# Performer attention and an MLP on one core: the seven-product form in all of block 7, a new sequence, and other engines for the scaled v rows

## The chip, the cores and the metric

One Trainium2 chip, one core of it. The kernel is a single launch: attention and the MLP that follows it, from the inputs in DRAM to the output in DRAM. The metric is device time in microseconds (us) of the slowest core, which here is the only one. Lower is better.

The engines are named as in the profile: PE is TensorE (PEld its weight loads), DVE is VectorE, ACT is ScalarE, POOL is GpSimd, SP is SyncE. SP, ACT and POOL issue DMAs.

## The reference

Eight batches (B), eight heads (H), 576 tokens (S), head size 64 (D), 128 random features (M). Attention is linear: queries and keys become positive features, and the keys are summed against the values once per head.

```python
def phi(x):
    proj = np.einsum('bhsd,md->bhsm', x, omega)
    sq = np.sum(x * x, axis=-1, keepdims=True) / 2.0
    h = proj - sq
    h = h - np.max(h, axis=-1, keepdims=True)
    return np.exp(h) / np.sqrt(m)

q_p, k_p = phi(q * D**-0.25), phi(k * D**-0.25)
kv  = np.einsum('bhsm,bhsd->bhmd', k_p, v)
z   = np.sum(k_p, axis=2)
num = np.einsum('bhsm,bhmd->bhsd', q_p, kv)
den = np.einsum('bhsm,bhm->bhs', q_p, z)[..., None] + 1e-06
x   = (num / den).transpose(0, 2, 1, 3).reshape(4608, 512)

h = x @ w_in                                   # 512 -> 2048
g = h * np.clip(h + 3.0, 0.0, 6.0) / 6.0
out = g @ w_out                                # 2048 -> 512
```

## The kernel before

**How the work is written down.** Each step is an `op` of a small planner (`Prog`): the engines that may do it, a cost, the function that emits its instructions, and the keys that it reads and writes. Steps have running numbers. A table `ORDER` lists, for each of the five engines, the numbers of its steps in sequence; an engine works its list strictly in that sequence. `schedule` replays the table with the planner's costs. It decides two things only: which of the eight PSUM banks a step gets, and how many fill matmuls (named `idle`, without use for the result) PE is given in the first 21 us (`IDLE_UNTIL`). `emit` turns the dependencies into semaphore waits. So the sequence on every engine is fixed ahead of the run, DMA issues included, and a step whose data are late holds up everything that is behind it on its engine.

**Attention, by batch.** A batch's 576 tokens are 512 main ones and 64 left over; pairs of heads share the 128 partitions. `load` (L619) issues the DMAs: in batch 0 SP and ACT issue k, q and v as f32 (pieces k00, k10, ..., q11, v11, and the left-over rows kl, ql, vl); in later batches POOL issues k and q as casting DMAs to bf16, and SP issues v. k and q are transposed (PE and DVE or ACT in batches 0 and 1, DMA from batch 2 on), PE projects them on omega (L808; L764 and L767 in the row-tiled form from batch 3 on), ACT takes the exponentials (L815, L783, L832, L792), and DVE takes the row maxima of the key features (L819, L788). The reciprocal of the maximum, `cc`, scales the v rows that belong to it:

- `vc` scales the 512 main rows of a pair of heads. On POOL it is one instruction (L924), on ACT eight (L926). `EV_VC` allows POOL or ACT in batches 1 to 7, `V0` gives POOL or DVE in batch 0.
- `vcl` (L851) scales the left-over rows, in two halves per batch: on DVE in batch 0, on POOL after it.

For each pair of heads PE then forms kv and z (L940, eight matmuls on `vc` and one on `vcl`, copied to `kvz`) and the numerator with its denominator (L968); DVE takes the reciprocal (L980) and divides (L984). The result goes to `xb` and is transposed to `xT`: by PE in batches 0 and 1, by a DMA that SP issues (L1013, `Xdma`) from batch 2 on. The left-over tokens of all batches are collected in `xS`.

**The MLP, by block.** Block b is the 512 main tokens of batch b; block 8 is the 8 x 64 left-over tokens. w_in comes in five casting DMAs from POOL (`w_in_piece`: wi0 in two parts, wi1, wi2, wi3, each 512 of the 2048 columns), gated by the landing of q11; w_out comes in eight. Block 0's first product is done in token halves (`mm1_half`, L1181). Blocks 1 to 8 use one of two forms for h = x @ w_in:

- `mm1` (L1037): for one of 16 column tiles four matmuls of 128 x 512, then a relu on ACT (L1043) and a multiplication on DVE (L1045).
- `mm1_pair`: two column tiles f and f+8 at once. The product is seen as a 2 x 2 by 2 x 2 block product and is done with seven block products for eight. PE issues 14 matmuls of 256 columns (L1116) in stages a, b, c, d. Between the stages are three copies on ACT (`s1` L1144, `s3` L1146, `s2` L1149) and two adds on DVE (`a2` L1152, `a1` L1154). The relu and the multiplication (L1163, L1165) follow twice.

The pair form needs sums of blocks of w_in (`input_sums`: W1 to W4, once per half of the column tiles, on DVE) and of x (`x_sums`: X1 to X4, once per block, on DVE or POOL). Which tiles use it is set by

```python
    FIRST7 = (8, 7)
    ...
    def seven(blk, f):
        return blk >= FIRST7[f // 4]
```

so in block 7 the pairs f = 4 to 7 use it and f = 0 to 3 do not; in block 8 all use it.

The second product, g @ w_out, of blocks 1 to 8 is in a seven-product form as well (`products`, L1290, outputs combined by `plus` L1306), on sums of w_out (T1 to T4) and on sums of g (`token_sums` and `last_sum`: S1 to S4, four groups per block). The sums of g, like those of x, go through `combine` (L1222); those of g are on POOL in every block. Block 0's second product is plain (L1206). The last product of block 8 is split into three parts so that its output leaves in pieces (`last_product`: L1356, adds C12.8 L1364, DMAs `outl` L1368). The other outputs leave by `store` (L1383).

**What sets the order around the change.** The table alone. The steps are interleaved far across batches: while PE works on block b, the engines prepare batches b+1 and b+2. In the first 21 us PE has little real work, since data are still landing, and the MLP of block 0 begins as soon as batch 0's first pairs of heads are through.

Of the kernel before, what the change touches and what calls it, by code (L numbers as in the profile page):

```python
# [15 lines left out]
EV0 = (("ACT","DVE"), ("ACT","DVE"), ("POOL","DVE"), {"k": ("POOL", "ACT", "DVE"), "q": ("POOL", "ACT","DVE")})  # L16
# [4 lines left out]
        13, 118, 139, 124, 150, 115, 144, 156, 162, 147, 153, 127, 121, 168, 133, 159, 130, 177, 175, 183, 136, 165,  # L21
        197, 212, 185, 199, 179, 142, 181, 219, 214, 204, 227, 202, 229, 171, 187, 242, 173, 217, 189, 232, 409, 415,
        244, 410, 411, 222, 207, 254, 416, 249, 257, 247, 417, 234, 403, 404, 405, 406, 412, 252, 418, 421, 237, 424,
        427, 430, 433, 436, 439, 282, 280, 442, 300, 303, 288, 445, 260, 448, 451, 284, 306, 286, 321, 454, 315, 312,
        318, 296, 309, 294, 457, 324, 292, 583, 290, 573, 574, 331, 339, 298, 329, 575, 584, 585, 343, 353, 337, 576,
        333, 327, 586, 577, 366, 341, 335, 587, 358, 355, 578, 379, 345, 368, 579, 371, 392, 588, 381, 394, 589, 397,
        384, 590, 374, 361, 593, 580, 387, 594, 400, 595, 596, 597, 621, 624, 630, 642, 627, 598, 636, 639, 654, 651,
        645, 657, 480, 599, 492, 666, 603, 477, 501, 604, 483, 605, 489, 672, 511, 660, 507, 600, 474, 503, 486, 606,
        505, 607, 513, 498, 509, 675, 517, 669, 495, 515, 608, 609, 782, 798, 610, 792, 539, 783, 519, 544, 527, 541,
        785, 529, 532, 786, 551, 793, 563, 695, 556, 553, 568, 795, 796, 565, 799, 702, 801, 802, 723, 805, 806, 709,  # L30
        809, 815, 812, 736, 818, 741, 824, 830, 827, 842, 833, 716, 839, 748, 863, 738, 860, 848, 854, 857, 845, 750,
        772, 980, 774, 760, 753, 970, 971, 762, 765, 986, 777, 973, 974, 981, 883, 890, 983, 984, 987, 897, 989, 990,
        911, 993, 1003, 997, 1000, 1012, 1015, 924, 1006, 926, 994, 1018, 929, 1021, 1030, 1027, 1033, 1042, 904, 936,
        1045, 1036, 1048, 1051, 938, 1168, 960, 1174, 941, 1158, 1159, 1071, 962, 948, 965, 1161, 1169, 950, 953,
        1162, 1171, 1078, 1172, 1175, 1085, 1177, 1178, 1092, 1181, 1191, 1185, 1112, 1194, 1200, 1117, 1188, 1203,
        1206, 1209, 1215, 1218, 1224, 1221, 1099, 1233, 1230, 1236, 1136, 1182, 1124, 1239, 1129, 1346, 1347, 1356,
        1148, 1126, 1114, 1349, 1141, 1138, 1153, 1150, 1350, 1357, 1362, 1287, 1359, 1259, 1360, 1363, 1266, 1365,
        1366, 1273, 1388, 1379, 1391, 1376, 1300, 1369, 1373, 1312, 1305, 1403, 1314, 1397, 1317, 1382, 1406, 1394,
        1302, 1336, 1409, 1412, 1338, 1370, 1421, 1418, 1424, 1280, 1427, 1341, 1534, 1535, 1544, 1454, 1537, 1538,
        1324, 1447, 1545, 1461, 1550, 1547, 1329, 1326, 1548, 1551, 1468, 1553, 1557, 1554, 1488, 1475, 1500, 1567,  # L40
        1502, 1490, 1558, 1579, 1493, 1512, 1561, 1505, 1524, 1591, 1576, 1526, 1514, 1517, 1570, 1529, 1582, 1600,
        1615, 1594, 1609, 1564, 1606, 1612, 1597, 1585, 1686, 1659, 1662, 1677, 1671, 1656, 1680, 1625, 1674, 1689,
        1699, 1626, 1691, 1665, 1702, 1628, 1694, 1635, 1704, 1629, 1715, 1636, 1707, 1728, 1718, 1641, 1720, 1638,
        1748, 1639, 1731, 1723, 1779, 1733, 1644, 1782, 1645, 1784, 1736, 1792, 1749, 1642, 1795, 1787, 1808, 1797,
        1648, 1811, 1649, 1800, 1821, 1813, 1751, 1824, 1752, 1826, 1816, 1837, 1758, 1829, 1850, 1840, 1759, 1853,
        1842, 1764, 1855, 1765, 1845, 1866, 1858, 1879, 1761, 1869, 1882, 1762, 1871, 1884, 1905, 1767, 1874, 1887,
        1768, 1895, 1771, 1772, 1896, 1911, 1906, 1898, 1899, 1908, 1909, 1912, 1915, 1916, 1924, 1932, 1928,
    ],
    "SP": [
        0, 21, 17, 22, 23, 32, 19, 24, 25, 31, 26, 27, 28, 29, 30, 269, 271, 270, 469, 470, 471, 468, 472, 473, 402,  # L50
        582, 467, 691, 692, 592, 602, 693, 694, 612, 547, 535, 690, 559, 689, 571, 688, 804, 572, 880, 879, 882, 808,
        881, 878, 756, 744, 877, 876, 768, 780, 781, 1067, 932, 992, 1069, 1064, 996, 1070, 1068, 1065, 968, 1066,
        944, 956, 969, 1180, 1255, 1256, 1258, 1184, 1257, 1253, 1120, 1144, 1132, 1252, 1156, 1254, 1368, 1157, 1440,
        1320, 1443, 1445, 1372, 1446, 1444, 1442, 1441, 1344, 1308, 1332, 1345, 1560, 1556, 1508, 1496, 1520, 1532,
        1533, 1647, 1651, 1774, 1770, 1918, 1935, 1927, 1931, 1930,
    ],
    "ACT": [
        18, 20, 123, 119, 140, 151, 145, 148, 163, 157, 129, 154, 135, 128, 134, 196, 141, 160, 211, 178, 166, 176,
        169, 184, 186, 226, 182, 180, 228, 241, 172, 203, 243, 190, 174, 188, 208, 223, 248, 407, 419, 413, 422, 425,
        253, 428, 238, 434, 431, 283, 437, 440, 443, 301, 304, 446, 449, 261, 452, 287, 307, 322, 316, 313, 310, 455,  # L60
        297, 293, 319, 352, 291, 325, 299, 458, 340, 344, 354, 378, 330, 365, 328, 332, 334, 338, 391, 336, 342, 346,
        380, 393, 388, 362, 401, 622, 625, 631, 581, 628, 640, 637, 643, 591, 655, 646, 481, 493, 658, 667, 502, 652,
        478, 484, 490, 512, 508, 661, 487, 475, 504, 506, 510, 514, 499, 518, 670, 516, 673, 537, 611, 676, 526, 540,
        496, 784, 520, 550, 561, 562, 787, 552, 564, 701, 696, 698, 705, 700, 708, 707, 703, 728, 724, 710, 712, 810,
        714, 715, 816, 746, 813, 819, 729, 825, 831, 726, 747, 828, 834, 719, 843, 717, 840, 721, 770, 849, 771, 855,
        759, 861, 846, 864, 722, 858, 972, 975, 886, 891, 884, 893, 888, 895, 889, 896, 900, 898, 902, 922, 914, 917,
        1004, 923, 998, 912, 1001, 1016, 1013, 916, 1007, 903, 1019, 1022, 1031, 1028, 1034, 1043, 905, 907, 1046,
        909, 1037, 958, 1049, 910, 1052, 946, 1160, 1072, 1074, 1077, 1076, 1163, 1081, 1083, 1079, 1084, 1086, 1090,
        1110, 1088, 1095, 1111, 1093, 1097, 1192, 1098, 1186, 1134, 1189, 1195, 1204, 1201, 1091, 1207, 1216, 1135,
        1210, 1219, 1225, 1222, 1234, 1105, 1100, 1237, 1102, 1231, 1125, 1146, 1240, 1348, 1137, 1104, 1288, 1290,  # L70
        1293, 1265, 1292, 1262, 1260, 1264, 1267, 1271, 1269, 1272, 1274, 1278, 1276, 1279, 1299, 1380, 1310, 1392,
        1377, 1374, 1313, 1335, 1389, 1383, 1404, 1398, 1395, 1337, 1410, 1407, 1413, 1422, 1419, 1425, 1283, 1281,
        1285, 1286, 1428, 1322, 1457, 1455, 1460, 1459, 1448, 1450, 1539, 1462, 1464, 1466, 1467, 1486, 1469, 1453,
        1452, 1474, 1471, 1473, 1499, 1478, 1476, 1511, 1481, 1568, 1523, 1480, 1580, 1513, 1562, 1525, 1571, 1583,
        1592, 1595, 1601, 1565, 1607, 1577, 1616, 1613, 1688, 1586, 1660, 1598, 1687, 1663, 1672, 1681, 1610, 1675,
        1657, 1690, 1700, 1701, 1627, 1695, 1666, 1703, 1678, 1630, 1717, 1716, 1697, 1710, 1719, 1708, 1729, 1724,
        1730, 1732, 1780, 1781, 1726, 1737, 1783, 1739, 1793, 1794, 1788, 1796, 1810, 1809, 1801, 1790, 1812, 1803,
        1822, 1823, 1817, 1825, 1819, 1839, 1830, 1838, 1832, 1851, 1852, 1841, 1854, 1753, 1859, 1848, 1846, 1868,
        1867, 1881, 1880, 1861, 1870, 1883, 1888, 1875, 1877, 1890, 1897, 1900, 1922, 1923, 1920, 1921, 1926, 1919,
        1934,  # L80
    ],
    "DVE": [
        16, 10, 7, 5, 12, 8, 11, 14, 138, 15, 4, 6, 125, 116, 152, 146, 149, 194, 122, 164, 155, 158, 191, 209, 192,
        193, 161, 224, 198, 131, 167, 213, 200, 170, 143, 239, 201, 215, 137, 220, 216, 230, 205, 231, 218, 206, 233,
# [316 lines left out]
def _emit(nc, es, q, k, v, omega, w_in, w_out, out):  # L401
# [109 lines left out]
    def dvet(n):  # L511
        return 0.07 + n / 960.0
# [508 lines left out]
    def mm1(blk, f):  # L1021
# [13 lines left out]
        def e(E):  # L1035
# [11 lines left out]
           t - 0.1, reads=[vh, ("t", tu)], writes=[("gT", gu, f, x) for x in range(2)], name="g.%d.%d" % (blk, f))  # L1047


    FIRST7 = (8, 7)  # L1050
    XADD = ("DVE", "POOL")
    AHEAD = 2
    LAG = 0.0
# [422 lines left out]
```

## Time and profile before

| | |
|---|---|
| Median of 4 runs | 308.24 us (307.27 to 309.17) |
| The profiled execution's own time | 309.17 us |
| Its span in the trace | 307.4 us |
| Granted TensorE clock, mean | 1.00 |
| Share of the span busy | PE 97%, DVE 79%, POOL 76%, ACT 70% |
| DMA | 44.88 MB, mean 146 GB/s |
| Fill matmuls | 56 |

The profiled execution is the slowest of the four; 1.8 us of its time lie outside the span. In a row of the groups, the first number behind the bar is the busy time of all instructions of that line and shape, the second the mean of one in nanoseconds; behind the second bar stands the engine's idle time just before them and what ended most of it. A row of the waits gives the waiting instruction, what ended the wait, and the time: sum, number, longest. A row of the chain gives the start, the length and the work. A row of the stages gives the interval, its length and for each engine the busy time with the number of instructions, then the granted clock, the mean share of the DMA engines and the GB/s.

### The profile page before, as it was taken

To read this page: it belongs to the slowest core of one execution; us is meant where nothing else is said; L and a number is where in the kernel's file an instruction comes from. 1 tells how busy PE (TensorE), PEld (TensorE's weight loads), DVE (VectorE), ACT (ScalarE), POOL (GpSimd) and SP (SyncE) were. 2 spreads that over 40 slices of the span, in tenths; PEclk is the share of its full clock that TensorE was granted. 3 is DMA by queue.
4 is the path that set the end of the run, shared out by engine and by line. 5 is a ranking of instruction groups with operands and counts; after the bars stand their busy time and mean duration, and the time that the engine had idled before them with its cause. 6 is when DMAs were issued, how large, how long until landed. Compare 5 with 4: busy or idle time off the path is not lost.

```text
span 307.4 us, 7302 instructions
## 1 busy us (share of the span) xinstructions
PE 298.8 (97%) x2767; PEld 209.7 (68%) x2767; DVE 242.3 (79%) x532; ACT 213.9 (70%) x518; POOL 232.7 (76%) x247
## 2 busy tenths in 40 slices
PE   7989999999998999999999999999999999999994
PEld 5767966445885468655864686557864478888883
DVE  3797898689886987788778878798698988978833
ACT  3886896579967984969699738769764766577410
POOL 2772769089895979889869894998941999899991
PEclk9999999999999999999999999999999999999999
DMA  8999998999799996499969996999834000030045
GB/s 223 272 167 177 265 195 126 207 210 170 178 174 185 131 227 159 95 137 210 228 176 121 146 218 137 152 162 227 126 139 78 2 0 2 1 139 1 2 162 113
DMA packets 90147, 44.88 MB, mean 146 GB/s; under 512 B 57984, under 2 KB 87808, under 8 KB 90112
## 3 DMA queue, kind: packets, MB, share of 16 engines
q1 hardware_dynamic: 62096, 30.68, 44.3%
q0 software_dynamic: 26592, 12.46, 32.8%
q10 hardware_dynamic: 1424, 1.28, 1.7%
q8 instruction: 22, 0.36, 0.5%
q14 instruction: 13, 0.11, 0.1%
HBM read 36.73 MB, written 9.44 MB: 150 GB/s over the span
## 4 chain that ended last, share of the span: by engine, by line
PE 81%; DMA 8%; DVE 5%; ACT 3%; issue 0%; SPq 0%; POOL 0%; DVEq 0%; POOLq 0%
PE p L1037 29%; PE p L1290 26%; PE p L1116 6%; PE p L1206 4%; PE p L1181 3%; DMA wi<-in_moe_w_in_dram 3%; PE p L968 3%; PE p L940 2%; DMA v<-in_v_dram 2%; PE p L808 2%; DMA xT<-xb 2%; PE p L764 2%; DMA k<-in_k_dram 2%; ACT vc L926 1%; PE p L828 1%; DVE mx L819 1%
## 5 line engine op out<-in xcount | busy, mean ns | idle before, releaser
L1037 PE MATMUL p<-xT,wi 128*128 128x512 f16 x416 | 96.2, 379 | 0.8 <-DMA xT<-xb 0.8
L1045 DVE SCALAR_TENSOR_TENSOR gT<-tsb,p 128x512 f16<-128x512 f16 x104 | 67.4, 678 | 14.1 <-ACT tsb L1043 13.3
L1043 ACT ACTIVATE tsb<-p 128x512 f16<-128x512 f32 x104 | 59.9, 599 | 24.2 <-PE p L1037 16.5
L1037 PEld LDWEIGHTS p<-xT,wi 128*128 128x128 f16 x416 | 39.2, 98 | 43.2 <-DMA xT<-xb 1.1
L1222 POOL TENSOR_TENSOR s<-gT 128x512 f16<-128x512 f16 x32 | 37.7, 1179 | 15.0 <-DVE gT L1045 12.1
L1290 PE MATMUL p<-wo,gT 128*128 128x256 f16 x368 | 45.9, 273 | 0.0
L1222 POOL TENSOR_TENSOR s<-gT,s 128x512 f16<-128x512 f16 x32 | 37.0, 1156 | 4.0 <-DVE gT L1045 1.8
L1222 POOL TENSOR_TENSOR gT<-gT 128x512 f16<-128x512 f16 x32 | 37.4, 1170 | 2.4
L1222 POOL TENSOR_TENSOR gT<-gT,s 128x512 f16<-128x512 f16 x32 | 37.3, 1165 | 2.5
L1290 PEld LDWEIGHTS p<-wo,gT 128*128 128x128 f16 x368 | 34.6, 98 | 5.2 <-issue 0.8
L788 DVE TENSOR_REDUCE mx<-kp 128x4 f32<-128x512 bf16 (+1 forms) x50 | 29.8, 623 | 7.2 <-ACT kp L783 7.0
L783 ACT ACTIVATE kp<-p 128x512 bf16<-128x512 f32 (+1 forms) x50 | 26.1, 554 | 12.6 <-PE p L767 11.9
L1290 PE MATMUL p<-t,gT 128*128 128x256 f16 x256 | 32.3, 273 | 0.0
L984 DVE TENSOR_TENSOR xb<-p,rec 128x256 f16<-128x256 f32 (+1 forms) x64 | 28.9, 471 | 0.6
L926 ACT ACTIVATE vc<-v,cc 128x64 bf16<-128x64 f32 x104 | 26.3, 347 | 2.5 <-DMA v<-in_v_dram 1.4
L792 ACT ACTIVATE qpT<-p 128x512 bf16<-128x512 f32 (+1 forms) x50 | 26.4, 562 | 2.2 <-PE p L968 2.1
L1290 PEld LDWEIGHTS p<-t,gT 128*128 128x128 f16 x256 | 24.3, 98 | 4.5 <-issue 0.8
L924 POOL TENSOR_TENSOR vc<-v,cc 128x512 bf16<-128x512 f32 x19 | 20.9, 1098 | 5.4 <-DVE cc L918 3.6
L619 POOL DMA_DIRECT2D qb<-in_q_dram x28 | 19.5, 706 | 3.3 <-DMA wi<-in_moe_w_in_dram 3.1
L1163 ACT ACTIVATE tsb<-p 128x512 f16<-128x512 f32 x24 | 14.0, 600 | 8.9 <-DVE p L1152 5.1
L968 PEld LDWEIGHTS p<-kvz,qpT 128*128 128x128 bf16 x312 | 15.3, 98 | 6.5 <-issue 0.3
L819 DVE TENSOR_REDUCE mx<-kp 128x4 f32<-128x512 bf16 x27 | 17.5, 674 | 1.9 <-ACT kp L815 1.8
(129 smaller groups left out, 552.6 us busy)
## 6 DMA issues: line engine op xcount, KB each, us to landing
v<-in_v_dram SPq DMA_DIRECT2D x14, 512.0 KB, 4.8
out_dram<-osb SPq DMA_DIRECT2D x14, 512.0 KB, 2.9
kb<-in_k_dram POOLq DMA_DIRECT2D x14, 256.0 KB, 4.9
qb<-in_q_dram POOLq DMA_DIRECT2D x14, 256.0 KB, 6.0
wo<-in_moe_w_out_dram POOLq DMA_DIRECT2D x8, 256.0 KB, 7.7
wi<-in_moe_w_in_dram POOLq DMA_DIRECT2D x3, 512.0 KB, 8.2
q<-in_q_dram SPq DMA_DIRECT2D x4, 256.0 KB, 5.6
vl<-in_v_dram SPq DMA_DIRECT2D x8, 128.0 KB, 4.5
```

What stands on the lines that cost most here:

```text
L783: op("ACT", actt(128 * (d1 - d0)), lambda E, lh=lh, ko=ko, part=part: E.activation(ko, out_of(part, 0, lh)[0].rearrange("p (x m) -> p x m" ...
L788: op("DVE", dvet(128 * (d1 - d0)), lambda E, ko=ko, mo=mo: E.reduce_max(mo, ko, axis=AX.X), p0 + 0.01, reads=[("kp", 0, d, lh) for d in ra ...
L792: op("ACT", actt(128 * (d1 - d0)), lambda E, lh=lh, part=part: E.activation(qd[:, part[0]:part[1], lh, :], out_of(part, 1, lh)[0].rearrang ...
L924: return E.tensor_tensor(vcm[:, :, 0:D], v32[:, m, :, :], cbc, ALU.mult)
L926: ins = E.activation(vcm[:, i, 0:D], v32[:, m, i, :], AF.Copy, scale=cc[pb][:, c0 + i:c0 + i + 1])
L968: ins = E.matmul(d[:, hh, i - i0, :], qpT[pb][:, o:o + 128], kvz[m][:, 65 * hh:65 * hh + 65], start=True, stop=True)
L984: op("DVE", dvet(128 * n), lambda E: E.tensor_tensor(xv(i0, i1), psum()[:, :, :, 0:64], rbc, ALU.mult), t + 0.01, reads=[vn, ("rec", ru)], ...
L1037: ins = E.matmul(ring.t[vh.slot], wi[:, c, 128 * f:128 * f + 128], xv[:, c, :], start=(c == 0), stop=(c == NJ - 1))
L1043: op("ACT", actt(512), lambda E: E.activation(tsb[tu][:], ring.t[vh.slot], AF.Relu, bias=0.5, scale=1.0 / 6.0), t - 0.1, reads=[vh], write ...
L1045: op("DVE", dvet(512), lambda E: E.scalar_tensor_tensor(gT[gu][:, f, :], tsb[tu][:], 1.0, ring.t[vh.slot], ALU.min, ALU.mult), t - 0.1, re ...
L1222: op(engines, {"POOL": 0.07 + n / 455.0, "DVE": 0.1 + n / 850.0}, lambda E: E.tensor_tensor(dst, x, y, ALU.subtract if minus else ALU.add) ...
L1290: ins = E.matmul(ring.t[v.slot][:, 256 * j:256 * j + 256], a[:, f, 128 * j:128 * j + 128], w[:, f, :], start=(first and f == 0 and j == 0) ...
```

## The change

It has five parts.

1. `FIRST7` becomes (7, 7): in block 7 the pairs f = 0 to 3 use the seven-product form too. The sums W1 to W4 of the first half are therefore needed before block 7 rather than before block 8, and the sums of x for block 7 are placed like those of block 8.
2. The copies s1, s2 and s3 of a pair may be on ACT or DVE (`EV_O`); a key `seed` keeps s3 behind s1. The dependency that held a pair behind the last stage of the pair before the last (`last7[-AHEAD]`) is left out.
3. `vcl` may be on POOL or ACT. On ACT it is four activations per half. `V0` allows POOL or ACT for `vc` in batch 0.
4. Sums of g of block 8, groups 2 and 3, may be on POOL or DVE; the new table puts five of them on DVE: S3 of groups 2 and 3, and S1, S2 and S4 of group 3. Five sums of x (X2 and X4 of block 7, X1, X3 and X4 of block 8) go from DVE to POOL.
5. The planner's latency for batch 0's loads is 1.4 us for 1.0 and their issue 0.52 for 0.47, and `ORDER` is a new table for all five engines. The number of fill matmuls that follows from it is 63 for 56. The store of block 7's first rows also reads the keys that the last adds of block 8 write, so that these wait for it.

```diff
-EV0 = (("ACT","DVE"), ("ACT","DVE"), ("POOL","DVE"), {"k": ("POOL", "ACT", "DVE"), "q": ("POOL", "ACT","DVE")})
+EV0 = (("ACT","DVE"), ("ACT","DVE"), ("POOL", "ACT"), {"k": ("POOL", "ACT", "DVE"), "q": ("POOL", "ACT","DVE")})
 ORDER = {
...
 }
@@ load
-               group="d" + part + ("c" if cast else "") + (str(pb) if b and part != "v" else ""), inc=16, lat=1.0,
-               name="%s.%d" % (part, b), issue=0.85 if cast else 0.47, packet=50.0 if run == 1024 else 18.0)
+               group="d" + part + ("c" if cast else "") + (str(pb) if b and part != "v" else ""), inc=16, lat=1.0 if b else 1.4,
+               name="%s.%d" % (part, b), issue=0.85 if cast else 0.47 if b else 0.52, packet=50.0 if run == 1024 else 18.0)
@@ attention
-            op(EV_V if b else V0, {"POOL": 0.72, "DVE": dvet(260)}, lambda E, hh=hh, p0=p0: E.tensor_tensor(
-                vcl[pb][p0:p0 + 64, :, 65 * hh:65 * hh + 65], vl[pb][p0:p0 + 64, :, :],
-                bass.AP(cc[pb], p0 * NCH, [[NCH, 64], [1, NP], [0, 65]]), ALU.mult), pos(1) + 0.04,
+
+            def e_vcl(E, hh=hh, p0=p0):
+                if E is not nc.scalar:
+                    return E.tensor_tensor(vcl[pb][p0:p0 + 64, :, 65 * hh:65 * hh + 65], vl[pb][p0:p0 + 64, :, :],
+                                           bass.AP(cc[pb], p0 * NCH, [[NCH, 64], [1, NP], [0, 65]]), ALU.mult)
+                for m in range(NP):
+                    ins = E.activation(vcl[pb][p0:p0 + 64, m, 65 * hh:65 * hh + 65], vl[pb][p0:p0 + 64, m, :], AF.Copy,
+                                       scale=cc[pb][p0:p0 + 64, m:m + 1])
+                return ins
+
+            op(("POOL", "ACT"), {"POOL": 0.72, "ACT": 0.9}, e_vcl, pos(1) + 0.04,
@@ mlp
-    FIRST7 = (8, 7)
+    FIRST7 = (7, 7)
@@ mm1_pair
-        op("PE", 2 * each, e_a, t, reads=[last7[-AHEAD]] + xkeys(blk, 0, 0) + [("X3", u), "W3%d" % (f // 4)] + klo,
+        op("PE", 2 * each, e_a, t, reads=xkeys(blk, 0, 0) + [("X3", u), "W3%d" % (f // 4)] + klo,
-        op("ACT", actt(256), lambda E: E.copy(half(V, 1), half(U, 0)), t - 0.1, reads=[U], writes=[V],
-           alloc=[V], name="s1." + nm)
-        op("ACT", actt(256), lambda E: E.copy(p7[w7][:], half(U, 1)), t - 0.09, reads=[U], writes=[("p7", w7)], name="s3." + nm)
+        op(EV_O, both(256), evac(lambda: half(V, 1), lambda: half(U, 0)), t - 0.1, reads=[U],
+           writes=[V, ("seed", blk, f)], alloc=[V], name="s1." + nm)
+        op(EV_O, both(256), evac(lambda: p7[w7][:], lambda: half(U, 1)), t - 0.09, reads=[U, ("seed", blk, f)],
+           writes=[("p7", w7)], name="s3." + nm)
-        op("ACT", actt(256), lambda E: E.copy(half(V, 0), half(V, 1)), t - 0.1, reads=[V], writes=[V], name="s2." + nm)
+        op(EV_O, both(256), evac(lambda: half(V, 0), lambda: half(V, 1)), t - 0.1, reads=[V], writes=[V], name="s2." + nm)
@@ token_sums, last_sum
+    def summing(blk, g):
+        return ("POOL", "DVE") if blk == 8 and g > 1 else ADD
+
-        combine("S3" + nm, S3[gu][:, r, :], a11, a21, True, 512, t, k11 + k21, [("S3", gu, g)])
...
+        eng = summing(blk, g)
+        combine("S3" + nm, S3[gu][:, r, :], a11, a21, True, 512, t, k11 + k21, [("S3", gu, g)], eng)
...
@@ store
+        if blk == 7 and i == 0:
+            keys += [("osb", j, 1, n) for j, n in ((0, 0), (1, 1), (1, 2))]
```

The start of the new table, beside the old one (names of the steps; `b` means batch 1's):

```
SP,   before  k left-over, k00, q00, q10, ql1, k01, q01, q11, ql0, v left-over, v00, v10, v01, v11
SP,   after   k left-over, k00, ql1, q10, q00, ql0, k01, q11, v left-over, v00, q01, v01, v10, v11
POOL, before  5 casts, wi0, wi1, wi0, vc.0.0, vc.0.1, vc.0.2, wi2, vc.0.3, wi3, kl b, k00 b, k10 b, ...
POOL, after   4 casts, wi1, wi0, wi0, vcl.0, vc.0.1, vcl.0, vc.0.0, wi2, vc.0.3, kl b, k00 b, wi3, k10 b, ...
```

## The prediction

> **What bounds the kernel now.** I read the page first, then the busy time by stages, then who PE waited for, and the chain of waits last.
>
> ```profile
> span 307.4 us, 7302 instructions
> PE 298.8 (97%) x2767; PEld 209.7 (68%) x2767; DVE 242.3 (79%) x532; ACT 213.9 (70%) x518; POOL 232.7 (76%) x247
> ...
> PEclk9999999999999999999999999999999999999999
> ...
> L1037 PE MATMUL p<-xT,wi 128*128 128x512 f16 x416 | 96.2, 379 | 0.8 <-DMA xT<-xb 0.8
> ```
>
> 97% alone would not prove much, since a busy PE need not be at its peak. The stages and the pace do:
>
> ```profile
> 10.00:21.00 11.00, 10.13 (x132) 8.15 (x131) 9.67 (x29) 9.88 (x24) 8.55 (x11) 1.00 1.05 203
> 21.00:40.00 19.00, 18.37 (x206) 16.05 (x203) 15.74 (x37) 14.66 (x33) 9.59 (x14) 1.00 1.30 217
> ...
> 230.00:250.00 20.00, 20.00 (x126) 10.84 (x125) 17.80 (x34) 12.36 (x25) 12.50 (x11) 1.00 0.19 36
> 250.00:270.00 20.00, 19.83 (x180) 17.25 (x178) 17.90 (x31) 11.93 (x29) 18.00 (x16) 1.00 0.04 17
> 270.00:290.00 20.00, 20.00 (x186) 17.93 (x184) 16.33 (x32) 13.32 (x32) 18.41 (x17) 1.00 0.10 38
> ```
>
> (After the interval: PE, weight loads, DVE, ACT, POOL, clock, DMA.) From 29 us to the last matmul at 302.7 PE runs without a break worth the name, and in the timeline four 512-column matmuls follow each other in 0.86 us and four 256-column ones in 0.44, at full clock. So there a microsecond of PE work is a microsecond of time. In 10 to 21 us PE's 10.1 is partly filler (56 fill matmuls in all); ACT, 9.9 of 11, is the full engine there.
>
> ```profile
> PE p L940 <- DVE vcl L851: 0.9, 1, 0.9
> PE p L1037 <- DMA xT<-xb: 0.8, 1, 0.8
> PE p L1181 <- DMA wi<-in_moe_w_in_dram: 0.6, 1, 0.6
> ...
> PE p L1116 <- DVE p L1154: 0.2, 1, 0.2
> ```
>
> These are PE's avoidable waits: vcl at 15.5 us, the last piece of w_in at 28.3 (start to start 0.80 too long), the transposed x of batch 2 at 95.9 (0.95 too long), the pair's sums at 251.8 (0.33). The chain shows what stood behind the first two:
>
> ```profile
> 14.53 0.53 DVE vcl L851
> 15.07 1.17 DVE vcl L851
> ...
> 19.61 0.99 POOL vc L924
> 20.59 8.42 DMA wi<-in_moe_w_in_dram
> 29.15 3.65 PE p L1181 x32
> ```
>
> **Seven products in all of block 7.** Four more pairs. Out: 32 matmuls of 512 at 0.216 = 6.9 us. In: 56 of 256 at 0.109 = 6.1. PE saves 0.8 us, all of it on the path. It costs 12 copies (0.38 each on ACT, some now on DVE) and 8 adds (0.43, DVE). In 230-250 DVE has 2.2 us free and ACT 7.6, so the 3.4 us of adds and the eight copies of both blocks that DVE now takes (about 0.4 each) fit only because five input sums (X2.7, X4.7, X1.8, X3.8, X4.8; 4.2 us by their rows) leave DVE for POOL. POOL has 7.5 us free in 230-250 but only 2.0 in 250-270; it gets five X sums of about 1.2 and loses five token sums of block 8 of about 1.17: even. The sums of w_in for the first half move ahead of block 7; W1 waits for block 6's last reader and by the new orders lies about 0.5 us ahead of the matmul that needs it. If that cover goes, PE waits for W1 (0.7 us).
>
> Here a rule speaks against the change. Row: a DVE sum of two SBUF inputs of 512 took 0.41 us alone, but X2.8 took 1.40 from 249.90, ending 0.28 after the POOL sum that ran from 249.87 to 251.02, and the 0.33 us PE wait came of it. The Trainium skill (SBUF — State Buffer, "SBUF: two separate sides") says that such a DVE instruction and a GpSimd one that reads SBUF hold a shared port as a lock, so one waits for all of the other; the trace agrees. By the quiet row the five token sums given to DVE cost 5 x 0.41 = 2.1 us of DVE; by the rule up to 5 x 1.4 = 7. DVE has 3.7 us free in 270-290 and most of 290-307, so a part could show: 0 to 1 us. The same lock explains vcl: 1.17 us from 15.07, ending 0.28 after POOL's vc (13.70-15.97). I take 0.3 us for all new waits together; bounds 0 (more room between a pair's stages, below) and +1.8.
>
> **The sequence.** (a) Batch 2's x: between its last numerator matmul and the first matmul of block 2 the old order has 7.0 us of PE work, the new 9.5. The wait of 0.95 should go: -0.9. Every other batch has at least 7.8 in the new order. What is late next: the vc steps behind a burst; the tightest distance from a burst to its kv product is 5.3 us (4.6 before, there with only 0.4 of delay). (b) Within the pairs the distance b to c stays at 0.87 us at the least, c to d at 1.5 (1.75 before). At zero.
>
> (c) The start. vcl moves from DVE to POOL (L851 on POOL: 617 ns) and one vc moves from POOL to ACT, eight instructions, 2.0 us by the chain's pieces "ACT vc L926 x8". SP sends q11 ahead of q01, one 256 KB piece (0.8 us of transfer) earlier, so POOL's w_in issues begin near 10.8 instead of 11.34; but they go second block first. POOL then has vcl, vc, vcl, vc, with cc of pair 0 late on DVE (about 16.5), so the third w_in issue comes at about 17.7 (18.32 before), and the last one behind vc, a k left-over and a k main piece: about 21.1 (20.59), and behind their bytes. In the old run those landed 0.44 and 1.36 us apart, after w_in. Landing: 29.0 - 0.6 + 1.8 = about 30.0.
> ACT: from its first unbroken exp (about 11.0) to vc it has 7.7 us of work (eleven exps of 512 at 0.49 us from start to start, two of 256 at 0.28, three casts and evacuations 1.3, four small copies 0.5), so vc runs 18.8-20.8, and the eQ and Xev behind it follow, which PE needs: kv.0.2 at 21.0, the first w_in matmul at about 22.7. PE's lag there (time less work done, filler apart) is 14.2-14.7 against 13.7 before. The matmul that needs the last piece has 14.7 us of work ahead of it (14.5 before): wanted at 29.4, data at 30.0. So PE leaves the start with a lag of 15.3-15.5 against 14.7: +0.8. Bounds: -0.8 (the data in time and ACT not the limit) and +2.5 (DVE's two casts blocked by POOL's instructions as above, which delays cc and so vc).
> The other price of an earlier vc, scaling on ACT in batches 1-7, is hidden: ACT loses 40 vc instructions and gains 20 vcl, POOL has 2.6 to 6.2 us free in each 30 from 70 to 220.
>
> (d) The end. Before, the last output went from SP at 304.76; now ACT issues six transfers and SP six; four of ACT's wait for the last C12 adds, and at 0.62-0.65 us each the last of them ends at about 305.5 instead of 305.39: +0.1. The guard on block 7's store adds a wait to the last adds of C12 for a transfer that ended 8 us earlier (293.4 issued): nothing.
>
> Sum: -0.8 - 0.9 + 0.8 + 0.1 + 0.3 = **-0.5 us**. The profiled run took 309.17 with a span of 307.4; its own time would be 308.7 and the span 306.9. It was the slowest of four; I apply the difference to the median: 308.24 - 0.5 = **307.7**.
>
> **Rivals.**
> 1. The start gains. For: vcl's 0.9 us wait goes, w_in's issue is earlier, the order was made for later transfers. Against: ACT is the full engine at 10-21 us and receives 2 us. If the k pieces don't hold up the last w_in (lag 13.9): -0.8 where I have +0.8, no new waits: -0.8 - 0.9 - 0.8 + 0.1 = -2.4: 305.8.
> 2. Slower: the last w_in piece, queued behind the two k pieces. Place: the wait at 28.3. At 30.0 it costs 0.6 us; each further microsecond is a microsecond of the end, because PE has no slack afterwards. From a landing past 31.0 or so the change is a loss; at 32.0, with 0.3 more elsewhere: +1.8, 310.0. For: one transfer of w_in took 8.4 us from its issue, and its issue is later. Against: the gap that DMA had at 20 us should close.
> 3. POOL becomes the bound of blocks 7 and 8, and the shorter PE work changes nothing. For: from 236.7 to 300.8 POOL ran 50 sums almost back to back, and PE's last product began at 300.95. Then -0.8 is lost: -0.5 + 0.8 = +0.3, 308.5. Against: five sums are on DVE at the very end.
> 4. The change does not do what it says: excluded for the counts (32 matmuls of 512 fewer, 56 of 256 more), so only its hiding can fail, which is 3.
>
> **How the numbers follow.** Forecast case 0.42, own range 306.2 to 309.2. Rival 1 0.26, rival 2 0.20, rival 3 0.12. A difference under 0.5% (1.5 us) is about what a measurement of this kernel can tell from none. Faster by more: most of rival 1 and the low edge of the forecast, 0.30. Slower by more: rival 2 and a little of the new waits, 0.22. Within: 0.48. The range takes rival 1 with its bounds (-3.0) and rival 2 (+2.2, a little beyond its price): 305.2 to 310.4.
>
> **What would show it.** PE in blocks 7: 384 matmuls of L1037's form instead of 416, and about 0.8 us less of PE work. Right if the wait on xT near 96 us is gone, ACT's first vc runs at 18.5-21, and the first matmul on the last w_in piece starts at 29.5-30.5. Rival 1 if it starts before 29; rival 2 past 31. DVE sums of block 8 should last 0.4 to 1.4 us, the long ones ending 0.3 us after a POOL sum. I am wrong if PE shows waits of more than 1 us in all after 31 us, or if POOL's last sum ends after PE could have begun the last product.

## Result and profile after

The changed kernel took 309.61 us in the median of 43 runs (307.29 to 313.42), the kernel before 308.15 us in 64 runs beside them: a ratio of 1.0031, with a 95% interval of 1.0018 to 1.0044. Forecast were 307.7 us, a small gain; it is a small loss. The ratio is not that of the two medians, which lie 1.5 us apart: it leaves disturbed runs out and puts the loss at about 1.0 us. The median lies inside the range that was given (305.2 to 310.4), on the wrong side of no change.

The page of the changed kernel's profiled execution, which took 311.14 us and so is at the slow end of its runs:

```profile
span 309.2 us, 7368 instructions
PE 298.4 (96%) x2798; PEld 211.0 (68%) x2798; DVE 245.8 (79%) x539; ACT 213.2 (69%) x511; POOL 234.0 (76%) x247
...
L1047 PE MATMUL p<-xT,wi 128*128 128x512 f16 x384 | 90.3, 379 | 0.5 <-DMA xT<-xb 0.5
...
L934 POOL TENSOR_TENSOR vc<-v,cc 128x512 bf16<-128x512 f32 x24 | 25.4, 1058 | 15.7 <-DVE cc L928 7.8
```

L1047 is the old L1037: 384 matmuls for 416, as the change says. PE is busy 0.4 us less than before and the span is 1.8 us longer, so PE stands still for longer. These are the instructions that PE waited with after 31 us (sum, number, longest); the kernel before had 0.8 us on xT and 0.2 on the pair's sums there:

```profile
PE p L950 <- POOL vc L934: 1.6, 2, 1.4
PE p L1305 <- POOL gT L1233: 0.8, 2, 0.6
PE p L1047 <- DMA xT<-xb: 0.5, 1, 0.5
PE p L1305 <- POOL s L1233: 0.3, 1, 0.3
```

The waits rose from 1.0 to 3.2 us, and all the new ones but that on the transposed x have POOL behind them. The busy time by stages shows where they lie (interval, length, PE, weight loads, DVE, ACT, POOL, clock, DMA):

```profile
10.00:21.00 11.00, 9.92 (x127) 7.61 (x127) 8.90 (x26) 10.22 (x31) 10.30 (x14) 1.00 1.17 230
21.00:40.00 19.00, 18.92 (x207) 16.52 (x205) 16.51 (x41) 15.44 (x33) 9.71 (x15) 1.00 1.33 224
...
130.00:160.00 30.00, 27.66 (x272) 17.61 (x269) 21.67 (x49) 20.08 (x47) 24.84 (x25) 1.00 1.08 176
160.00:190.00 30.00, 29.98 (x297) 19.94 (x296) 23.31 (x51) 21.79 (x51) 27.35 (x30) 1.00 1.04 159
190.00:220.00 30.00, 29.30 (x272) 18.48 (x268) 23.98 (x56) 22.98 (x59) 25.05 (x26) 1.00 0.89 164
...
250.00:270.00 20.00, 19.85 (x182) 17.53 (x181) 18.44 (x39) 13.40 (x32) 18.75 (x17) 1.00 0.07 28
270.00:290.00 20.00, 20.00 (x185) 17.82 (x184) 19.33 (x39) 12.67 (x30) 18.62 (x17) 1.00 0.07 27
```

In 130 to 160 us PE lacks 2.3 us. The kernel before lacks nothing there:

```profile
130.00:160.00 30.00, 30.00 (x292) 19.74 (x290) 23.40 (x53) 23.54 (x62) 25.24 (x27) 1.00 1.06 183
```

The start is better than before (18.92 of 19.00 in 21 to 40 us for 18.37), and PE is as full as before in block 7 (250 to 290 us). The granted clock is 1.00 in all these stages, so the loss is not one of the clock.

The chain of waits between 128 and 146 us shows the place, and something that is easily misread:

```profile
128.43 0.75 POOL qb L621
129.18 3.52 issue
...
132.74 1.05 POOL vc L934
...
133.93 0.42 PE p L950 x8
...
144.27 1.16 POOL gT L1233
...
145.57 2.78 PE p L1305 x24
```

"issue" for 3.52 us reads as if POOL had waited for nothing. The timeline of the same stretch names what it was, on POOL and on SP (start, length, work, and in brackets the idle time with its releaser):

```profile
132.74 1.04 POOL L934 TENSOR_TENSOR vc<-v,cc 128x512 bf16<-128x512 f32 x1 [3.57 <-DMA v<-in_v_dram]
```

```profile
124.04 0.58 SPq L621 DMA_DIRECT2D v<-in_v_dram  x1
124.67 1.20 SPq L886 DMA_TRANSPOSE xS<-xb  x1
125.91 0.58 SPq L621 DMA_DIRECT2D v<-in_v_dram  x1
126.54 0.50 SPq L1400 DMA_DIRECT2D out_dram<-osb  x1
```

POOL stands idle 3.57 us before `vc.4.0` because v of batch 4 is not there. SP sends its second piece, v10, at 125.91; it lands 6.8 us later, at 132.7. The new table had moved it. This is SP's order around it, by the steps' names (Tdmaq and Tdmak transpose q and k, Xdma and Sdma transpose x, outw stores an output, vl is the left-over v; the number is the batch or block):

```
before  ... Tdmaq.4.0, v10.4, Xdma.3.1, Xdma.3.0, v00.4, vl.4, Xdma.3.2, Xdma.3.3, Sdma.3, Tdmak.5.0
after   ... Tdmaq.4.0, outw.1.1, vl.4, Xdma.3.1, Xdma.3.0, outw.1.0, Xdma.3.2, Xdma.3.3,
            Tdmaq.4.1, v00.4, Sdma.3, v10.4, outw.2.1, Tdmak.5.0
```

In the kernel before, v10.4 went out at 114.13 us, and there the wait does not exist:

```profile
114.13 1.17 SPq L619 DMA_DIRECT2D v<-in_v_dram  x1
```

PE pays more than once: 1.42 us at `kv.4.0`, which needs that `vc`, then 0.64 us at the product P3.4 at 145.57 and 0.28 at 151.65, because POOL's sums of g of block 3 stand in the list behind the `vc` that waited. That is 2.3 us, all that PE lacks in this stage.

The stages alone don't give PE's lag, which the prediction used: the start of a matmul less the work ahead of it, filler apart, each matmul at its unhindered pace. It is summed from the trace's records and stands in no view. Its size depends on the pace set for the row-tiled bursts, so only the difference between kernels at the same matmul is read:

| at the matmul | before | after | after with v early (below) |
|---|---|---|---|
| last of block 0's first half (mm1.0A.14), near 30 us | 14.68 | 13.81 | 13.71 |
| num.3.3A, near 113 us | 15.09 | 13.80 | 13.70 |
| mm1.6.7, near 238 us | 12.21 | 14.38 | 10.92 |
| first of the last eight matmuls (302.27, 304.00, 300.56 us) | 12.64 | 15.16 | 11.72 |

So the changed kernel was 1.3 us ahead at 113 us. It then lost 3.5 us against the kernel before until 240 us and another 0.35 to the end, and it had 0.8 us less work. Together that is a loss of 1.7 us, which is the difference of the last starts (304.00 and 302.27).

### The profile page after: what moved, and what is told of

It is laid out like the page before. It is cut to its first block, busy times and chain, and to the rows that moved or that the text cites. A ratio compares the mean times of both kernels' runs of the same rounds, so it can differ in the third digit from the quotient of the medians.

```text
span 309.2 us, 7368 instructions
## 1 busy us (share of the span) xinstructions
PE 298.4 (96%) x2798; PEld 211.0 (68%) x2798; DVE 245.8 (79%) x539; ACT 213.2 (69%) x511; POOL 234.0 (76%) x247
## 4 chain that ended last, share of the span: by engine, by line
PE 66%; POOL 20%; DVE 4%; DMA 3%; issue 3%; SPq 2%; ACT 1%; POOLq 0%
PE p L1305 22%; PE p L1047 21%; POOL gT L1233 8%; POOL s L1233 7%; PE p L1192 5%; PE p L1217 4%; PE p L978 3%; PE p L950 3%; PE p L766 2%; DMA q<-in_q_dram 2%; PE p L830 1%; POOL vc L934 1%; DMA v<-in_v_dram 1%; SPq L621 1%; PE p L769 1%
## 5 line engine op out<-in xcount | busy, mean ns | idle before, releaser
L1047 PE MATMUL p<-xT,wi 128*128 128x512 f16 x384 | 90.3, 379 | 0.5 <-DMA xT<-xb 0.5
L1055 DVE SCALAR_TENSOR_TENSOR gT<-tsb,p 128x512 f16<-128x512 f16 x96 | 62.8, 679 | 12.5 <-ACT tsb L1053 11.8
L1047 PEld LDWEIGHTS p<-xT,wi 128*128 128x128 f16 x384 | 35.4, 98 | 38.7 <-issue 1.1
L1233 POOL TENSOR_TENSOR gT<-gT,s 128x512 f16<-128x512 f16 x31 | 35.9, 1157 | 5.2 <-PE p L1305 2.9
L1233 POOL TENSOR_TENSOR s<-gT 128x512 f16<-128x512 f16 x30 | 34.9, 1162 | 6.4 <-DVE gT L1055 4.3
L1233 POOL TENSOR_TENSOR gT<-gT 128x512 f16<-128x512 f16 x31 | 36.1, 1166 | 2.4
L934 POOL TENSOR_TENSOR vc<-v,cc 128x512 bf16<-128x512 f32 x24 | 25.4, 1058 | 15.7 <-DVE cc L928 7.8
L522 ACT COPY p<-p 128x256 f32<-128x256 f32 (+1 forms) x46 | 17.7, 398 | 14.0 <-PE p L1126 5.6
L1174 ACT ACTIVATE tsb<-p 128x512 f16<-128x512 f32 x32 | 18.8, 598 | 6.5 <-PE p L1126 3.9
L621 POOL DMA_DIRECT2D kb<-in_k_dram x21 | 16.5, 786 | 7.4 <-PE p L1047 7.4
L1321 DVE TENSOR_TENSOR u<-p 128x512 f32<-128x512 f32 x16 | 11.0, 688 | 13.5 <-PE p L1305 13.4
```

The costliest lines, as they stand in the source:

```text
L621: lambda E: E.dma_start(dst, src), prio + 0.001 * turn_of[0], reads=gate, writes=keys,
L934: return E.tensor_tensor(vcm[:, :, 0:D], v32[:, m, :, :], cbc, ALU.mult)
L1047: ins = E.matmul(ring.t[vh.slot], wi[:, c, 128 * f:128 * f + 128], xv[:, c, :], start=(c == 0), stop=(c == NJ - 1))
L1055: op("DVE", dvet(512), lambda E: E.scalar_tensor_tensor(gT[gu][:, f, :], tsb[tu][:], 1.0, ring.t[vh.slot], ALU.min, ALU.mult), t - 0.1, re ...
L1174: op("ACT", actt(512), lambda E, v=v, tu=tu: E.activation(tsb[tu][:], v.ring.t[v.slot], AF.Relu, bias=0.5, scale=1.0 / 6.0), t - 0.1, read ...
L1233: op(engines, {"POOL": 0.07 + n / 455.0, "DVE": 0.1 + n / 850.0}, lambda E: E.tensor_tensor(dst, x, y, ALU.subtract if minus else ALU.add) ...
```

## The experiments

Each run is compared with runs of the kernel before on the same chip. The edits of `ORDER` use one helper:

```python
def _move(eng, n, ahead_of):
    order = ORDER[eng]
    order.remove(n)
    order.insert(order.index(ahead_of), n)
```

### Is it v, sent late by SP?

The theory is that SP's new place for v10.4 made the loss. The rival is that POOL simply has too much: 24 `vc` instructions for 19, beside the sums.

```diff
+_move("SP", 877, 882)  # v00.4 ahead of Tdmaq.4.1
+_move("SP", 878, 882)  # v10.4 ahead of Tdmaq.4.1
```

> The changed kernel, with one edit: SP issues the two v pieces of batch 4 (v00, v10) right behind the last xT transpose of batch 3, ahead of q's second transpose and of Sdma.3, so v10 goes out at about 123.3 us for 125.9. Theory (v late): in the changed kernel vc.4.0 on POOL sat idle 3.57 us until v landed at 132.7, PE lost 1.4 us at kv.4.0, and POOL's sums behind it, 3.5 us late, cost PE another 1.0 (P3.4 0.6 to 0.8, P3.2 0.2 to 0.3). So both waits go: -2.2 us against the changed kernel's profiled run, somewhat less at the median (its profiled run was the slow end of its runs): ratio to before about 0.996 to 0.999 where the changed kernel has 1.003. Rival (POOL has too much vc and vcl work, 24 and 11 instructions for 19 and 14): the waits on L1233 near 145 to 152 us stay, and at most 1.4 goes, or the kv.4.0 wait comes from cc.4.0 (127.3) or POOL's own DMA issues and stays.

Measured: 307.88 us against 309.27 of the kernel before, ratio 0.9957 (0.9938 to 0.9976). The same edit was run a second time, on another chip:

> The changed kernel with both v pieces of batch 4 early, again, as the base for the run beside it. Both theories: 0.994 to 0.998.

Measured: 0.9965 (0.9941 to 0.9990). These are the waits after 31 us in the second run, and the timelines of POOL and of SP in the first:

```profile
PE p L960 <- POOL vc L944: 0.2, 1, 0.2
PE p L1315 <- POOL s L1243: 0.2, 1, 0.2
PE p L1315 <- POOL gT L1243: 0.2, 1, 0.2
```

```profile
129.13 0.74 POOL L631 DMA_DIRECT2D qb<-in_q_dram  x1 [0.88 <-DMA qT<-qb]
129.89 1.06 POOL L944 TENSOR_TENSOR vc<-v,cc 128x512 bf16<-128x512 f32 x1
```

```profile
122.01 1.13 SPq L631 DMA_DIRECT2D v<-in_v_dram  x2
123.18 1.53 SPq L757 DMA_TRANSPOSE qT<-qb  x1
```

`vc.4.0` starts without idle time, 2.85 us earlier, and the waits at 133, 145 and 152 us are gone, with POOL as full as in the changed kernel (234.0 us busy in both). The wait on xT at 191 us is gone too, although nothing was done for it. The rival falls: POOL's load is the same, and it was only held up by v.

The smallest form of the edit:

```diff
+_move("SP", 878, 781)  # v10.4 ahead of Sdma.3
```

> The changed kernel with the smallest edit: SP issues v10 of batch 4 one place earlier, ahead of Sdma.3, 1.25 us sooner. Theory: POOL's idle time before vc.4.0 falls by 1.25 us, to 0.4 to 2.3, and PE's waits there by at least half: ratio 0.997 to 1.001, between the changed kernel's and that of the run with both v pieces early (0.996). Rival (it is the second transpose of q, moved with them in that run, that mattered): as the changed kernel, 1.003.

Measured: 0.9967 (0.9944 to 0.9990), as with both pieces early. One step moved by one place is worth all of it, and the rival, q's second transpose, which stayed where it was, is out. Its timeline:

```profile
123.39 1.16 SPq L630 DMA_DIRECT2D v<-in_v_dram  x2
124.60 1.17 SPq L895 DMA_TRANSPOSE xS<-xb  x1
```

Here the slower of the two pieces landed 5.2 us after its issue, where v10 took 6.8 us in the changed kernel. So 1.25 us in the sequence brought more than 1.25 us, and the expected rest of 0.4 to 2.3 us of idle time did not come. That the transfer now gets ahead of POOL's k and q loads of batch 5 (issued from 126.25 us on in the changed kernel) would explain it; no run isolates that.

The changed kernel itself once more, on the chip of those two runs:

> The changed kernel itself, on the chip of the three runs beside it, for a second profile. Theory (v late, by a landing that varies from execution to execution: v10 took 6.8 us to land in the first profile and 5.4 in the run with FIRST7 (8, 7), with POOL idle for 3.57 and 1.61 us before vc.4.0): POOL idles 1.5 to 3.6 us before vc.4.0 again, PE's waits between 130 and 153 us come to 0.6 to 2.7 us, ratio to before near 1.003. Rival (the first profile was a chance and the typical execution loses its time elsewhere): no idle time before vc.4.0, and other waits of 2 us or more after 31 us.

Measured: 309.94 us, ratio 1.0037 (0.9999 to 1.0074), against 307.96 with v early on the same chip. Its profile, an execution at its slowest end (313.16 us):

```profile
134.20 1.04 POOL L934 TENSOR_TENSOR vc<-v,cc 128x512 bf16<-128x512 f32 x1 [4.61 <-DMA v<-in_v_dram]
```

```profile
PE p L950 <- POOL vc L934: 2.7, 2, 2.5
PE p L950 <- POOL vcl L856: 0.6, 1, 0.6
```

The landing took 7.2 us. In three executions of this SP order (this one, the first, and the one with `FIRST7` undone below) it took 7.2, 6.8 and 5.4 us, and POOL stood for 4.61, 3.57 and 1.61. All three are slower than the median of their kernel, so the typical wait may be shorter than the first profile shows. That the changed kernel's time varies with this landing fits: it spreads from 308.57 to 313.16 us in these 12 runs, and with v early on the same chip from 307.59 to 309.54. Three profiles do not prove it. The wait of 0.6 us for a `vcl` of the next batch, at 168 us, is in this profile and in the one with `FIRST7` undone, and in none with v early.

The reverse, in the kernel before:

```diff
+_move("SP", 877, 1067)  # v00.4 behind Sdma.3
+_move("SP", 878, 1067)  # v10.4 behind v00.4
```

> The kernel before, with one edit, the reverse of the first: SP issues both v pieces of batch 4 behind Sdma.3, at about 125.7 and 126.3 us, where it issued them at 114.1 and 120.2. Theory: v lands at 131 to 133, and PE waits about 1.5 us at the kv products of batch 4, more if POOL's sums then queue behind the vc: +1.5 to +2.5 us, ratio 1.005 to 1.008. Rival (the order on POOL and not v makes the wait): within 0.5 us of before, 1.000 to 1.0015.

Measured: ratio 1.0208 (1.0176 to 1.0239), +6.3 us: the direction as expected, the size three times too small. In the kernel before, a `vc` of batch 4 is on ACT. The timelines of ACT and PE, the waits of PE and two stages (as above) tell what stood behind it:

```profile
131.31 2.02 ACT L936 ACTIVATE vc<-v,cc 128x64 bf16<-128x64 f32 x8 [5.29 <-DMA v<-in_v_dram]
133.23 0.57 ACT L793 ACTIVATE kp<-p 128x512 bf16<-128x512 f32 x1
```

```profile
PE p L1047 <- ACT kp L793: 4.4, 1, 4.4
```

```profile
133.86 5.30 PE L1047 MATMUL p<-xT,wi 128*128 128x512 f16 x12 [4.35 <-ACT kp L793]
```

```profile
130.00:133.00 3.00, 0.00 (x0) 0.00 (x0) 0.00 (x0) 1.69 (x8) 2.32 (x3) 1.00 1.11 164
136.00:139.00 3.00, 3.00 (x9) 1.07 (x8) 1.28 (x2) 0.38 (x1) 1.23 (x3) 0.50 0.59 109
```

The exponentials of the next burst wait behind the `vc`, their PSUM banks stay full, and PE stops for 4.4 us at a matmul that needs no v at all. On POOL the late v held up sums that had more room.

The stop is not the whole price. After it the granted clock is 0.50: the twelve matmuls from 133.86 us take 0.43 us each from start to start for 0.22, which is 2.5 us more, and up to 139.9 us another 0.4 is lost. Stop and slow matmuls are 7.3 us together, where this execution took 7.5 us longer than the profiled one of the kernel before (316.71 and 309.17). In that one the clock is 1.00 in the same stretch.

The two cases of a late v differ in more than the engine: ACT stood for 5.29 us here and POOL for 3.57 there. So the runs show that the price depends on what is queued behind the instruction that waits, and on how PE runs after its stop; they do not give a price per engine for the same lateness.

### The start

> The kernel before, with the changed kernel's first 31 us only: vcl on POOL, vc.0.2 on ACT, SP's and POOL's new order of the loads, q11 ahead of q01, wi1 ahead of wi0; from there on the old sequence, and seven products as before. Theory (the start is a gain and stays one): the changed kernel's PE stood 0.84 us earlier at 31 us, so -0.84 us, ratio 0.9973, and a wait at vcl near 15.5 us and at wi near 28.3 that are gone. Rival (what the start gains is given back at the wait on xT near 96 us, whose data come by DMAs): PE stands earlier at 31 us and not at 100, ratio 1.000. Rival of the prediction (the last w_in piece late): slower than before.

```diff
-EV0 = (("ACT","DVE"), ("ACT","DVE"), ("POOL","DVE"), {"k": ...
+EV0 = (("ACT","DVE"), ("ACT","DVE"), ("POOL", "ACT"), {"k": ...
+            op(("POOL", "ACT"), {"POOL": 0.72, "ACT": 0.9}, e_vcl, pos(1) + 0.04,   # with e_vcl of the change
 ORDER = {
...   # on each engine: the changed kernel's steps before 31 us, then the others in the old sequence
```

Measured: 1.0001 (0.9979 to 1.0023). The expected 0.9973 is just outside, and neither -0.5 us nor no change is excluded. In its profile PE's lag is 14.10 at the end of the first half of block 0 for 14.68, 14.19 near 113 us for 15.09, 11.10 for 12.21 near 238, and 12.14 for 12.64 at the last matmul. So a gain of about 0.6 us appears in the start, is kept and reaches 1.1 by 238 us; half of that goes again up to the end, where PE waits on DVE for 0.4 and 0.2 us in block 7, the old kernel's tight place. That is one execution; the timing does not confirm the gain. The rival of the prediction, a late last piece of w_in, has nothing for it: PE does not wait for w_in here.

### The seven products

`FIRST7` back to (8, 7), the rest of the new order as it is:

```diff
-    FIRST7 = (7, 7)
+    FIRST7 = (8, 7)
 ORDER = {
...   # mm1.7.f for stage b of the pair, mm1.7.(f + 8) for stage d; W1 of the first half ahead of a2.7.5
```

> The changed kernel with its first part undone: FIRST7 is (8, 7) again; the four matmuls of mm1.7.f stand where stage b of the pair stood and those of f + 8 where stage d stood, W1 of the first half goes behind them, the rest of the new order stays. Theory (the seven products save PE time and all of it is on the path): +0.8 us against the changed kernel, ratio to before 1.005 to 1.007 where that has 1.003. Rival (POOL or DVE bounds blocks 7 and 8, so that PE's saving is lost): 1.003, with the sums of block 8 ending at the same distance from the end.

Measured: 1.0021 (1.0000 to 1.0041). The theory's 1.005 to 1.007 is missed, but the execution in its profile had a shorter landing of v than the changed kernel's, and no wait at `kv.4.0`; a difference of 0.5 us can't be read beside that. So the comparison was made once more, with v early on both sides:

> The run above with FIRST7 (8, 7), so that the seven products are measured without v's varying landing. Theory (PE's saving of 0.8 us is on the path, less about 0.3 of new waits on POOL's sums): slower than the run above by 0.5 us, 0.15%. Rival (the saving is lost to POOL): equal within 0.1 us. The timing alone can hardly part these; the profile can: the time from the first matmul of block 6 to the last matmul, less its work, against that of the run above.

Measured: 308.34 us, ratio 0.9990 (0.9966 to 1.0014), against 307.96 and 0.9965: 0.4 us slower, not certain by the timing alone. From mm1.6.7 to the last matmul its lag grows by 0.53 us and with the seven products by 0.80, for 0.79 us less work: a net gain of 0.5 us. The prediction's 0.8 less 0.3 is what the two traces show; the timing alone excludes neither that nor nothing.

### POOL at the end

> The changed kernel with v of batch 4 early on SP, S47.1 ahead of S18.2, and the five sums of block 8 that it gave to DVE back on POOL. Theory (POOL at its limit in blocks 7 and 8, DVE has the room): POOL's last sums end about 2 to 3 us later than PE needs them, so PE waits 2 to 3 us on L1233's sums after 285 us: ratio to before 1.002 to 1.006, against 0.995 with the sums on DVE. Rival (the shared-port rule: the DVE sums cost as much as they relieve): within 0.3% of that 0.995.

```diff
 # with v early and S47.1 ahead of S18.2
+for n, ahead_of in ((1891, 1893), (1920, 1929), (1921, 1929), (1922, 1929)):  # S38.2, S38.3, S28.3, S18.3 from DVE
+    ORDER["DVE"].remove(n)
+    ORDER["POOL"].insert(ORDER["POOL"].index(ahead_of), n)
+ORDER["DVE"].remove(1932)
+ORDER["POOL"].append(1932)  # S48.3 from DVE, behind S48.2
```

Measured: 1.0144 (1.0097 to 1.0191), some 5.5 us slower than with v early alone, twice what was expected. PE's waits after 285 us, the matmuls behind the longer one and a stage there:

```profile
PE p L1321 <- POOL s L1249: 2.9, 2, 2.6
```

```profile
294.77 1.14 PE L1321 MATMUL p<-t,s 128*128 128x256 f16 x8 [2.64 <-POOL s L1249]
295.71 3.52 PE L1321 MATMUL p<-wo,gT 128*128 128x256 f16 x16
```

```profile
296.00:298.00 2.00, 2.00 (x11) 1.40 (x10) 0.65 (x1) 0.00 (x0) 0.29 (x1) 0.50 0.00 0
```

The lag grows by 5.0 us from P7.6 on. The waits of 2.9 us in it are what was expected. No later product waits: the rest is the clock, which is 0.50 after the stop of 2.6 us. The sixteen matmuls from 295.71 us take 3.36 us to the start of the next for 1.74 with v early alone, 1.6 us more. So POOL had no room for all of these five sums, which take 5.8 us there at 1.16 us each; its lateness itself is 2.9 us of the loss, and the clock behind the stop 1.6. That DVE takes them is not an ornament of the change; with the five sums of x on POOL, it carries it. On DVE they cost 4.2 us, here in the changed kernel's profile:

```profile
286.44 1.25 DVE L1233 TENSOR_TENSOR s<-gT 128x512 f16<-128x512 f16 x1
292.83 1.08 DVE L1233 TENSOR_TENSOR s<-gT 128x512 f16<-128x512 f16 x1
294.44 0.77 DVE L1233 TENSOR_TENSOR s<-gT,s 128x512 f16<-128x512 f16 x1
295.74 0.41 DVE L1233 TENSOR_TENSOR gT<-gT 128x512 f16<-128x512 f16 x1
300.78 0.71 DVE L1233 TENSOR_TENSOR gT<-gT,s 128x512 f16<-128x512 f16 x1
```

```profile
285.02 2.38 POOL L1233 TENSOR_TENSOR gT<-gT 128x512 f16<-128x512 f16 x2
...
291.25 3.68 POOL L1233 TENSOR_TENSOR s<-gT,s 128x512 f16<-128x512 f16 x3
297.60 3.62 POOL L1233 TENSOR_TENSOR gT<-gT,s 128x512 f16<-128x512 f16 x3 [2.66 <-PE p L1305]
```

The one of 0.41 ran while POOL stood idle (294.93 to 297.60). The first ended at 287.69, 0.28 us after the POOL sum that ended at 287.41; the other three likewise 0.27 to 0.29 behind one. What the prediction read from two pairs of rows shows in four more.

### Attempts at more

```diff
 # with v early
+_move("SP", 1254, 1157)  # v10.6 ahead of Sdma.5
+_move("SP", 1180, 1157)  # outw.3.1 behind v10.6
+_move("SP", 1252, 1180)  # vl.6 behind v10.6
```

> The run above, and the same kind of edit near 181 to 190 us: SP issues v10 of batch 6 ahead of Sdma.5, and outw.3.1 and vl.6 behind it, so the four xT transposes of batch 5 end about 1.2 us earlier. Theory (SP's sequence): the xT wait at mm1.5.1 (0.5 to 0.65 us) and the kv.6.0 wait (0.2 to 0.4) go: a further -0.9 us, ratio to before about 0.994 to 0.996. Rival (these waits are DMA time, not issue time): the landing of xT comes no earlier, and the sum stays within 0.3 of the run above.

Measured: 0.9986 (0.9967 to 1.0006), not better than with v early alone (0.9957), and the profile shows a new wait. The expectation was taken from the changed kernel, whose xT wait at 191 us had already gone with the first edit. The new wait, at 192 us, is on an add into the output buffer, which fits the store `outw.3.1`, now later, keeping that buffer longer:

```profile
PE p L1060 <- DVE osb L1334: 0.6, 1, 0.6
```

```diff
 # with the edits above
+_move("POOL", 1783, 1893)  # S47.1 ahead of S18.2
```

> The run above, and on POOL the sum S47.1 ahead of S18.2, one place: S47.1 ends 1.2 us earlier. Theory: P7.6 no longer waits for it (0.3 us) and nothing else is late, since S18.2 has 10 us: a further -0.3, within the noise of the timing; the wait on L1233 near 291 us is gone from the profile. Rival (POOL is the bound of blocks 7 and 8): the 0.3 us come back at the next sum.

Measured: 0.9966 (0.9951 to 0.9982). The wait at P7.6 (0.32 us from start to start, 0.2 in the list of waits) is gone from the profile and does not come back before the end; the timing can't part this from the run above with certainty.

```diff
 # with v early
+_move("POOL", 1298, 1434)  # vc.6.0 ahead of k10.7
+_move("POOL", 1803, 1620)  # X1.8 behind S26.3
+_move("DVE", 1804, 1737)   # X2.8 ahead of a2.7.5
+_move("POOL", 1783, 1893)  # S47.1 ahead of S18.2
```

> The changed kernel with v of batch 4 early on SP, and three one-place edits for the waits that its profile still shows: on POOL vc.6.0 ahead of the issue of k10 of batch 7 (kv.6.0 waited 0.39 us), X1.8 behind S26.3 with X2.8 later on DVE (P6.2 waited 0.33), S47.1 ahead of S18.2 (P7.6 waited 0.32). Theory (all PE time after 31 us is on the path, each wait is worth its length): -1.0 us against the run with v early alone, ratio 0.992 to 0.994. Rival (each such wait comes back at the next late sum, POOL being nearly full): 0.995 to 0.997.

Measured: 0.9965 (0.9947 to 0.9983). The three waits are gone or smaller (from start to start 0.39, 0.33 and 0.32 became 0, 0.11 and 0), but there is a new one at P7.4 for a sum of block 7 (0.45 in this measure, 0.3 in the list). The lag at the last matmul is 11.15 for 11.72: 0.6 us, where 1.0 was expected, and nothing that the timing shows. Of the versions that beat both kernels, the one with a single step moved does as well as any.

## Why the prediction was wrong

- **The step that failed** is (a) of the sequence, with its answer to "What is late next". It found every other batch's x in time and took "the vc steps behind a burst" for the tightest place, by PE work between burst and kv product. The other operand of `vc`, v, was not followed on SP, though the change moved it there from ahead of four x transposes to behind them, behind q's second one and behind Sdma.3. So it stood in the sum at nothing, without a reason. What the runs show in its place: v10.4 goes out at 125.91 us for 114.13, POOL stands for 3.57 us and PE for 2.3 us in that execution. Moved ahead again it is worth -2.3 us by the ratios (1.0031 to 0.9957) and -2.0 on one chip (309.94 to 307.96); with it in place the change is a gain of 1.0 to 1.3 us.
- **Two errors of opposite sign.** Without the late v the forecast of -0.5 would have been too small, since the start was put at a loss (below). That the median lies inside the stated range is no merit of the argument: that side of the range was made for rival 2, a late last piece of w_in, and the loss came from elsewhere.
- **The x wait of batch 2** went, as said. It was worth 0.4 us by the lag (from -0.87 at 30 us to -1.29 at 113), 0.8 by its row, for 0.9. The prediction took the start-to-start excess in full.
- **The start** had the wrong sign. +0.8 was summed; the changed kernel's profile shows -0.87, and the start alone in the old kernel -0.6. The term that was mis-sized is ACT's `vc`, put at 18.8 to 20.8: the timeline has it at 17.71 to 19.74, and the first matmul on w_in at 21.96 for the 22.7 that was expected. The last piece of w_in did not hold PE up at all in that execution (the matmul on it at 28.51, wanted at 29.4 by the prediction). It did by 0.4 to 0.7 us in four of the ten other profiles of the changed kernel and its versions; one of these is the changed kernel's second, whose lag at 30 us is still 0.5 less than before. Rival 1 had this part right: a start before 29, and -0.8.
- **The seven products** were right: 0.8 less work, and 0.5 net by the traces. The waits of 0.3 us from start to start at P6.2 and P7.6 on POOL sums are what took the rest, and the kernel before had 0.3 of its own at 252 us.
- **POOL in blocks 7 and 8** was sized rightly as even, and rival 3 (POOL becomes the bound) did not come in. But the run with the sums back on POOL shows that it stood on the edge: PE then waited 2.9 us, and at the halved clock behind that it lost another 1.6.
- **The end**: from the start of the last eight matmuls to the end of the span it is 5.1 us before and 5.2 after. +0.1 was right.
- **Scaling on ACT and POOL in batches 1 to 7**, called hidden, is hidden once v is in time: 0.2 us of waits on `vc`. With v late it is not a matter of load but of what stands behind it.
- The test "PE shows waits of more than 1 us in all after 31 us" was the one that told: 3.2 us. The right terms (-0.8 for the work, -0.87 for the start, -0.42 for the x wait, +0.35 in the end) sum to -1.7 us, and with v early the last matmuls start 1.7 us earlier than before.

## What to carry to other kernels

When a sequence is replaced, follow each consumer's every operand to its issue on each queue, not only the ones that had been late: a load that moves a few places on a busy DMA-issuing engine is a new wait, and the sum over engine loads can't show it. Price a wait by what is queued behind the waiting instruction on its engine, and then look at the granted clock behind every stop of PE: a stop of 4.4 us cost about 7. After a fix read the waits anew before mending the next one, since some were only its echo.

## What had not been expected of the hardware

The same v piece took between 5.4 and 7.2 us from issue to landing in three executions of the same SP order, and the slower of the two pieces 4.9 to 5.2 us in four executions with v10 going out one or more places sooner. A transfer's landing varied by more than the whole effect that was to be measured.

Stops of PE were followed by a granted clock of 0.50 in two runs, after 4.35 us and after 2.64 us. The longest stop of the changed kernel's second profile, 2.47 us, was not: the clock stays at 1.00. What decides between them no run here isolates.

A chain that calls 3.52 us of POOL "issue" can hide a DMA wait: the timeline's bracket named it.
